# Gates taken from their PSUM banks, and a new order of work, in the seven-product ReGLU tiles of an attention and FFN kernel

## The chip, the core and the metric

One Trainium2 chip; the kernel runs on one of its cores. The metric is the time of one execution on the device in microseconds. The engines are TensorE (PE; PEld are its weight loads), VectorE (DVE), ScalarE (ACT), GpSimd (POOL) and SyncE (SP, which here issues transfers only). Each engine works through its own queue in the order written, and waits on semaphores of others. A transfer is issued from an engine's queue and lands later.

## The reference

Eight batches of eight heads, 576 positions of 64 numbers, attention that is causal by blocks of 64, and then a ReGLU feed-forward layer on all 4608 rows of 512 numbers, with 1536 hidden units:

```python
pos = np.arange(S)
mask = (pos[:, None] // 64) >= (pos[None, :] // 64)
scores = np.where(mask, q @ k.T * D ** -0.5, -1e9)
attn = softmax(scores)                       # per batch and head
x = (attn @ v).transpose(0, 2, 1, 3).reshape(B * S, H * D)
gate = np.maximum(x @ w_gate, 0.0)
val = x @ w_val
return (gate * val) @ w_out
```

## The kernel before, in words

**Tiles.** The 4608 rows go through the feed-forward layer as nine tiles of 512 columns: tiles 0 to 7 are the first 512 positions of the eight batches, tile 8 holds the 64 last positions of each. While tile j is in the feed-forward layer, the attention of the next batch runs between its matmuls. Tiles 0 to 2 have an order of their own that the change leaves alone. Tiles 3 to 6 share one text, `ORDER_3_6`; tiles 7 and 8, which have no attention beside them, have `ORDER_7` and `ORDER_8`. `program(j)` (L1324) turns each token of such a text into instructions; the order of tokens is the order on every engine's queue. No planner runs: order, banks and the sharing between engines are tables written out in the file.

**Seven products.** From tile 3 on a pair of hidden quarters (128 units each, two per pair) is computed with Winograd's form of Strassen's method: seven products of half size instead of eight. Token `pNw` is product w of pair N (L1363, four matmuls of 256 columns in two tokens). Products 1, 6, 5, 3 go to one PSUM bank (`w_`), 7 and 4 to another (`v_`), 2 to a third (`x_`). Between products the running sums are taken out: `pNa`, `pNu`, `pNw` are ScalarE copies of a bank to SBUF (L1385), `pNd`, `pNe`, `pNc` are VectorE additions of a bank to such a copy (L1389). At the end the bank `w_` holds the gate of the upper half of the columns, the copy `a` that of the lower half, `u` and `w` the values. The two hidden products are

```python
elif what == "r":
    relu((n, "high"), st[n, "w_"])        # ScalarE, L1334: gate_sb <- bank
...
if gate is not None:                      # L1401, VectorE or GpSimd
    on(name).tensor_tensor(out=h[:, :, at], in0=split(gate), in1=val, op=AX.mult)
else:                                     # L1405, VectorE: max(gate, 0) * value
    nc.vector.scalar_tensor_tensor(out=h[:, :, at], in0=split(...), scalar=0.0, in1=val, ...)
```

`pNL` is the lower half (always L1405, both inputs in SBUF). `pNH` is the upper half: with a token `pNr` before it, the ReLU copies the gate to SBUF and L1401 multiplies; without it, L1405 reads the PSUM bank itself. GpSimd can only do the form of L1401.

**Other tokens.** `g`, `v`, `r`, `h` are hidden quarters without the seven products (512-column matmuls L1339, ReLU L1334, VectorE product L1435). `X`, `Y` are sums of the input halves that pairs need (L1171), `sQPKK` sums of hidden quarters (L1020), `U` sums of weights (L979, in tile 6 only). `M1` to `M7` are the seven output products of a tile (L1061, six tokens each) over all twelve quarters; `oa`, `ou`, `ow`, `oy` are their ScalarE copies (L1106), `od`, `oe`, `oc` VectorE additions (L1100), `S0` to `S3` and `P` the stores (L893), on ScalarE's queue. In tile 8 the last parts are halved (`oya`, `oyb`, `oca`, `ocb`, L1118; stores `Sa`, `Sb`, `Sya`, `Syb`, two 64-row blocks after another, on several queues, L906). For attention, `A` is a visit (scores of two heads, L631, in banks of all three pools), `E` its exponentials (t, u, f of 512 columns, L643, or s of 1024, L636), `C` zeroed corners (memset L1519 on GpSimd, L1516 on VectorE), `V` the products with v (L779, L793), `N` the normalisation (L716, L718, L725), `T` the transposing transfer of the result to `xT` (L862, SyncE's queue; `T3` also issues that of the last positions, L765), `K` and `k` the last keys, `l` and `w` loads of a later batch (GpSimd's queue, L509), `d0` to `d3` the transposing transfers of its q and k (SyncE's queue, L519, L524, L526). `l`, `w` and `d` are left out in tile 6.

**Banks and queues.** PSUM has eight banks: two tiles `sc` of two banks, of which a pair uses the first, one bank `one`, three banks `ffnp`. `PAIR_BANK`, `OUT_BANK` and `AV_BANK` say which pool each accumulation uses, `SLOTS` which buffer of the pool, one after the other. A bank's next user on TensorE waits until ScalarE and VectorE have read it. `ON_POOL` lists the operations that GpSimd does; the rest of their kinds fall to VectorE (`on`, L946).

Of the kernel before, what the change touches and what calls it, by code (L numbers as in the profile page):

```python
# [17 lines left out]
def kernel(  # L18
# [91 lines left out]
    ORDER_8 = """  # L110
        p01 p31 p01 p0a p17 p11*2 p1a X4 p07 p17 p07 p0w p06 p12 p06 p0u p12 p1c p16*2
        p04 p05*2 p0d p21 p1u p15*2 p31 p1w p1d p14*2 p1e p3a p04 p1L p0e p21 p2a p03*2
        p0r p0H p13 p02 p13 p1r p02 p0c P p1H p36 p26*2 p2u p27*2 p2w p41 p32 p25 p32
        p41 p4a p25 s0002 p0L s0102 p2d p3c p37*2 p3w p36 p3u p24*2 p2e p23*2 p2r p2H
        p34*2 p3e p35 p47 p35 p3d p22*2 p47 p2c p4w p3L p2L p42 p51*2 p5a p42 p33*2 p3r
        p3H p4c p46*2 p56 p44*2 p4u p4e p4L p56 p5u p57*2 p5w p45*2 p4d p55*2 p5d p54*2
        p5e M2 p52 p43 p52 p5c p5L p53 p43 p4r p4H p53 p5r p5H M1*2 M2 M1*4 M2*4 s0202
        s1002 s1202 oa s2002 s2202 M6*2 M7 s2102 M6*4 s1102 M7 s0302 s2302 M7*4 ou oca
        Sa M5*5 ocb s1302 Sb ow M5 od M4 S2 M4*3 M3*3 oya Sya M4*2 oe S1 M3*3 oyb Syb
# [25 lines left out]
        (4, 2): ('one', 'sc', 'ffn'),  # L145
        (4, 3): ('ffn', 'sc', 'ffn'),
# [2 lines left out]
        (5, 2): ('one', 'sc', 'ffn'),
        (5, 3): ('ffn', 'sc', 'ffn'),  # L150
# [2 lines left out]
        (6, 2): ('one', 'sc', 'ffn'),
        (6, 3): ('ffn', 'sc', 'ffn'),
# [12 lines left out]
        (8, 5): ('ffn', 'ffn', 'sc'),  # L167
# [1649 lines left out]
```

## Time and profile before

| | |
|---|---|
| time, median of 3 runs | 345.14 us (344.94 to 345.31) |
| the profiled execution's own time | 344.71 us |
| its span | 342.8 us, granted TensorE clock 0.997 |
| TensorE busy | 332.7 us (97%) |
| VectorE, GpSimd, ScalarE busy | 233.1, 216.7, 210.8 us |

Read the busy shares with the stages in mind: tiles 3 to 6 take some 35.7 us each (tile 4 from about 174.5 to 210.2 us, tile 5 to 245.8), tile 7 runs from about 281.4 and tile 8 from about 309.3 us. Times in the views are from the start of the span; an operation's duration overlaps the next one's start on its engine, so the rate of a full queue is read from starts, not from durations. Idle time in square brackets is that of the engine before the row, with what released it.

### The profile page before, as it was taken

The numbers are of one execution on the slowest core, as the hardware profiler recorded it, in microseconds if no ns is written. First come the engines' busy times: TensorE is split into PE (matmuls) and PEld (weight loads), VectorE is DVE, ScalarE is ACT, GpSimd is POOL, SyncE is SP. The second block draws the span as 40 slices with busy tenths as digits, with TensorE's granted clock in tenths as the row PEclk, the third lists the DMA queues.
The fourth block names the chain that finished last, engine by engine and source line by source line (L and its number), as shares of the span: only waits on it lengthen the run. The fifth ranks groups of instructions, "written<-read, shape, count | busy, mean of one in ns | idle before, by whom it ended". The sixth has DMA issues, their size and how long they took to land.

```text
span 342.8 us, 8917 instructions
## 1 busy us (share of the span) xinstructions
PE 332.7 (97%) x3477; PEld 233.8 (68%) x3518; DVE 233.1 (68%) x540; ACT 210.8 (61%) x344; POOL 216.7 (63%) x272
## 2 busy tenths in 40 slices
...
GB/s 242 294 351 371 368 230 238 240 163 155 187 197 137 144 158 137 165 143 121 111 165 120 130 116 153 128 137 118 138 33 2 33 122 12 2 31 94 33 0 122
DMA packets 155337, 50.06 MB, mean 146 GB/s; under 512 B 134496, under 2 KB 151648, under 8 KB 155296
## 3 DMA queue, kind: packets, MB, share of 16 engines
...
## 4 chain that ended last, share of the span: by engine, by line
PE 88%; issue 4%; DVE 2%; ACT 2%; POOL 2%; POOLq 0%; DVEq 0%; ACTq 0%
PE ffnp L1179 16%; PE ffnp L1363 9%; PE ffnp L1339 8%; PE sc L1363 8%; PE sc L1061 6%; PE ffnp L1282 6%; PE ffnp L1061 6%; PE one L1363 5%; PE one L1061 4%; PE sc L631 3%; PE one L631 2%; PE one L779 2%; PE ffnp L779 2%; PE one L1179 2%; PE sc L779 1%
## 5 line engine op out<-in xcount | busy, mean ns | idle before, releaser
L636 ACT ACTIVATE attnT<-sc 128x1024 bf16<-128x1024 f32 x56 | 56.7, 1036 | 0.0
L1189 ACT ACTIVATE gate_sb<-ffnp 128x512 bf16<-128x512 f32 x35 | 20.6, 599 | 27.3 <-PE ffnp L1179 24.4
L1179 PE MATMUL ffnp<-xT,wg 128*128 128x512 bf16 x130 | 36.2, 379 | 0.6
L1061 PEld LDWEIGHTS <-stage 128*128 128x128 bf16 x336 | 32.0, 98 | 4.1 <-issue 0.2
L1363 PEld LDWEIGHTS <-stage 128*128 128x128 bf16 x288 | 27.3, 98 | 7.8
L779 PEld LDWEIGHTS <-attnT 128*128 128x128 bf16 x640 | 26.3, 98 | 7.7 <-DVE xnat L718 1.2
L1179 PE MATMUL ffnp<-xT,wv 128*128 128x512 bf16 x108 | 31.3, 380 | 0.2
L1199 DVE TENSOR_TENSOR hT<-gate_sb,ffnp 128x512 bf16<-128x512 bf16 x28 | 19.2, 684 | 14.9 <-PE ffnp L1179 12.0
L1389 DVE TENSOR_TENSOR ob<-ffnp,ob 128x512 f32<-128x512 f32 x29 | 19.8, 684 | 12.6 <-ACT ob L1385 12.6
L509 POOL DMA_DIRECT2D v_bf<-in_v_dram x30 | 24.3, 829 | 6.0 <-PE sc L793 3.1
L1061 PEld LDWEIGHTS <-hT 128*128 128x128 bf16 x252 | 24.2, 98 | 5.3 <-DVE hT L1405 1.1
L1363 PEld LDWEIGHTS <-wg 128*128 128x128 bf16 x224 | 21.9, 98 | 5.1
L1363 PEld LDWEIGHTS <-wv 128*128 128x128 bf16 x224 | 21.5, 98 | 5.3 <-ACT attnT L636 1.1
L1106 ACT COPY ob<-sc 128x512 f32<-128x512 f32 x13 | 7.6, 586 | 28.4 <-PE sc L1061 27.0
L1519 POOL MEMSET attnT<- 64x256 bf16 x34 | 10.2, 314 | 23.4 <-ACT attnT L636 16.0
L1282 PE MATMUL ffnp<-wo,hT 128*128 128x512 bf16 x91 | 23.1, 379 | 0.2
L1179 PEld LDWEIGHTS <-wg 128*128 128x128 bf16 x144 | 13.3, 98 | 13.8 <-issue 0.5
L1179 PEld LDWEIGHTS <-wv 128*128 128x128 bf16 x144 | 13.0, 98 | 14.3 <-issue 1.5
L1334 ACT ACTIVATE gate_sb<-ffnp 128x512 bf16<-128x512 f32 x30 | 17.6, 603 | 8.1 <-PE ffnp L1363 4.6
L509 POOL DMA_DIRECT2D q_bf<-in_q_dram x20 | 18.0, 908 | 5.0 <-DVE recip L752 4.0
L643 ACT ACTIVATE attnT<-one 128x512 bf16<-128x512 f32 (+1 forms) x28 | 15.0, 537 | 9.8 <-PE ffnp L631 8.4
L1020 POOL TENSOR_TENSOR stage<-hT,stage 128x512 bf16<-128x512 bf16 x15 | 17.4, 1167 | 4.2 <-DVE stage L1020 3.6
...
## 6 DMA issues: line engine op xcount, KB each, us to landing
...
stage<-in_moe_w_out_dram SPq DMA_DIRECT2D x6, 512.0 KB, 10.5
...
```

The source lines that it names most:

```text
L509: ins = nc.gpsimd.dma_start(dst, part_of)
L636: return lambda: nc.scalar.activation(at[:, :, lo : lo + 512], sc, AF.Exp, scale=scale)
L779: nc.tensor.matmul(av[:, p, :], at[:, col : col + 128], v_bf[b % 2][:, c, h, :], start=(p == 0), stop=(c == p), skip_group_check=True,)
L1061: nc.tensor.matmul(to, sums.of(c)[which][:, 128 * p : 128 * p + 128], right, start=first, stop=(c == 5), skip_group_check=True,)
L1179: nc.tensor.matmul(to, (wg, wv)[t][f // 4][:, c, 128 * (f % 4) : 128 * (f % 4) + 128], x[:, c], start=(c == 0), stop=(c == 3),)
L1189: nc.scalar.activation(gate_sb, gate, AF.Relu)
L1199: nc.vector.tensor_tensor(out=h, in0=gate_sb, in1=val, op=AX.mult)
L1282: nc.tensor.matmul(op, hT[f][:, 128 * s : 128 * (s + 1)], wo[f // 4][:, f % 4, n0:n1], start=(f == 0), stop=(f == 11),)
L1334: nc.scalar.activation(st[key], of, AF.Relu)
L1339: nc.tensor.matmul(to, (wg, wv)[t][f // 4][:, c, 128 * (f % 4) : 128 * (f % 4) + 128], x[:, c], start=(c == 0), stop=(c == 3),)
L1363: nc.tensor.matmul(st[key][:, 256 * k : 256 * k + 256], left[:, c, 128 * k : 128 * k + 128], right[:, c], start=new and (k, c) == (0, 0), ...
L1389: nc.vector.tensor_tensor(out=t, in0=st[n, of], in1=t, op=AX.add)
```

## The change

No function changes, only the tables.

1. The tokens `p1r` in tiles 3 to 6, `p1r`, `p3r`, `p4r`, `p5r` in tile 7 and `p1r`, `p4r`, `p5r` in tile 8 are gone. The upper halves of these pairs are now L1405 on VectorE with the gate's PSUM bank as an input; ReLUs that stay are `p3r` and `p5r` in tiles 3 to 6 (pair 2 had none before), `p0r` and `p2r` in tile 7, `p0r`, `p2r`, `p3r` in tile 8.
2. `ON_POOL` is shared out otherwise: in tiles 3 to 6 one upper half, two corners and two input sums leave GpSimd, and the hidden sums it takes are others; the weight sums, tile 7 and tile 8 change likewise.
3. Seven accumulations move from the `sc` banks to the `ffnp` banks, and many others change place. `SLOTS` is written anew from tile 3 on: `sc` has 126 places instead of 133, `ffnp` 233 instead of 226, `ob` 96 as before, `gate_sb` 65 instead of 76.
4. The three orders are written anew. In tiles 3 to 6 the second visit (`A1`) comes later, behind `p35`; the transposing transfers go out as T0 T1 d0 d1 d2 d3 T2 T3 instead of d0 d1 T1 T0 d2 d3 T2 T3; the loads `w4` and `w5` come earlier. In tile 7 `M7` comes ahead of most of `M1`. In tile 8 `M7` and `M1` come ahead of `M2`, and the store `Sb` moves behind `oya`.

The diff shows tile 3 for tiles 3 to 6 in the tables, grouped by tile:

```diff
--- before
+++ after
@@ -43,40 +43,39 @@
     SLOTS = {
...
     ORDER_3_6 = """
-        l0 A0 E0t E0u g0*2 p12 w0 p12 X5 X7 E0s E0f X6 X4 K g0*2 g1*2 p11*2 p1a g1*2
-        p17*2 p16*2 C00 C01 p1c k V00 N00 P v1*2 p1u p15*2 p1w p1d p14 V01 N01 p14 p1e
-        p1L v1*2 r0 r1 p13*2 p1r v0*2 h1 A1 E1t v0*2 h0 p21*2 E1s p22*2 w1 p27*2 p2a
-        p26*2 E1u l1 w2 p31 p1H l2 l3 p2c p31 g8 U05 l4 p2w p24*2 w3 s0002 p2u p2e p2L
-        l5 l6 p25 g8 p25 p2d C11 p3a p36*2 p32 p37*2 E1f C10 V11 l7 N11 U06 l8 p3u p35
-        p3w p35 p3d g8*2 r8 p23*2 p2H l9 p34*2 p3e p33*2 p3r p32 A2 E2t E2u p3c p3L v8*4
-        h8 p57 p51*2 p57 p52 E2s V10 N10 p5a p56*2 p5w d0 d1 T1 p5u s0202 p3H p52 p5c g9
-        p54*2 p5e l10 s1102 g9*3 p55*2 p5d C21 p5L s1002 E2f r9 s0302 s1202 A3 E3t v9
-        E3f U45 s0102 p53*2 p5r C20 v9 V21 v9 N21 v9 M1 h9 V20 M1*2 p5H s2102 s2002 E3s
-        C30 N20 U47 M1*3 M7*2 T0 d2 d3 E3u C31 V30 M7 V31 N30 T2 oa N31 s2202 s2302 M6*6
-        ou M7*3 ow M2 M5*5 M4 M5 M4*3 od S2 M4*2 oe S1 M2 U46 U43 M3 U07 w4 s1302 M3*5
-        M2*4 oc oy S0 w5 T3 U03
+        A0 E0t l0 X5 E0s E0u C01 X7 X6 g1*4 g0 E0f C00 K g0 p11*2 p1a g0 w0 w1 X4 p12*2
+        p1c g0 l1 w2 l2 p17*2 p16*2 k V00 N00 v1*4 P r1 p1u p1w h1 r0 p15*2 p1d V01 N01
+        p21 p14 p21 p2a p14 p1e v0 p27 v0*3 U05 h0 p1L p13 p26*2 p13 p1H p27 p22*2 p2c
+        p31 g8 p2w p24 p2u p24 p2e p31 p3a p25*2 p2d g8 p37*2 p3w p2L p36*2 p23*2 p2H
+        p34*2 g8 p3u p3e g8 r8 l3 l4 p35 w3 l5 l6 l7 A1 E1t l8 E1s U45 s0002 E1u C11 p35
+        p3d v8 E1f p32*2 p3c v8*3 h8 U06 s0202 p33*2 p3r p51*2 A2 E2u C10 V11 E2t p3L
+        p52*2 N11 p57*2 p5a p56 p5c V10 w4 p3H s1002 E2s s1102 p5w p56 p5u T0 N10 T1 d0
+        g9*2 C21 p54*2 p5e g9 E2f p55*2 p5d g9 U03 d1 d2 l9 l10 d3 r9 A3 E3u E3s p53*2
+        v9 p5L v9 s0102 s1202 v9*2 M1*2 p5r M1*2 E3f M1 M7 M1 h9 p5H s2002 C20 w5 E3t
+        C31 V21 C30 M7 V20 V30 N21 oa M6 s2202 M6*4 s2102 N30 N20 T2 M6 ou V31 N31 T3
+        M7*2 M2 M7*2 ow M5 M2 M5*5 od S2 M4*3 s0302 U46 M4*3 oe s1302 S1 U47 U07 M3
+        s2302 M3*5 M2 U43 oy M2*3 oc S0
     """
     ORDER_7 = """
-        p11 X5 X7 X6 X4 p01*2 p0a p02*2 p11 p1a p0c p12*2 p1c p06*2 p16*2 p07*2 p17*2
-        p0u p05*2 p21 p0w p1u p21 p04*2 p0d p0e p2a p15*2 p1w p1d p22 p03 p22 p03 p0r
-        p31 p14*2 p13*2 p1r p26 p31 p0L p27 p26 p27 p2c p1e p1H Y5 p1L p37*2 p0H s0002
-        s0202 s0102 p32*2 p2u p25 p3a p3c p36 p25 p36 p2w p24*2 p2d p2e p51*2 p3w p3u
-        p35*2 p3d p23*2 p2L p34*2 p5a p56 p33*2 p2r p2H p3e p3L p52 p57 p56 p41 p57 p41
-        p47 p3r p3H p52 p5c p42*2 p5u p55 p4a p4c p46*2 p47 p55 p5w p54 p5d p54 p5e M1
-        s1002 s1202 s1102 p4w p4u p44*2 p4e p45 p53 p45 p4d p53 M1 p5r P p4L p5L p5H
-        M2*2 M7 p43 M7 p43 p4r p4H s2002 s2202 s2302 M1*4 oa M2*4 M6*6 s2102 M7*4 ou
-        M5*3 ow M5*3 od S2 oc M4*6 s1302 s0302 oe M3*4 S1 Y7 Y6 M3*2 oy S0
+        p11 X5 X7 p01*2 p0a p21 p12 p11 X6 X4 p12 p1a p1c p07 p06*2 p0u p07 p02*2 p0c
+        p16 p05*2 p0w p0d p16 p1u p04*2 p0e Y5 p0L p17 p21 p2a p03 p17 p1w p15 p03 p15
+        p26 p14*2 p1d p31*2 p1e p1L p13 p0r p0H p3a p27 p22 p27 p2w p22 p2c p26 p13 p37
+        p1H s0002 s0202 p24*2 p36 p2u p2e p25 p37 p25 p51 p32 p36 p32 s0102 p51 p2d p23
+        p52 p2L p3c p3u p35*2 p23 p52 p3w p3d p34*2 p5a p5c p2r p56 p57 p56 p33*2 p5u
+        p3e p57 p41*2 p42*2 p4a p3H p2H s1002 p5w p3L p4c p47*2 p55 p46 p55 p5d p46
+        p54*2 p5e p4w p44 p4u p44 p4e p45*2 p4d p4L M1 s1102 p53 M7*2 p53 p43 M2 p43 M2
+        M1 p5L M1*4 M2*4 oa s1202 M6 p5H p4H s2002 s2202 s2302 M6*5 ou P s2102 M7*4 ow
+        oc s0302 M5*5 s1302 M5 od Y7 S2 M4*6 oe S1 M3*6 oy S0 Y6
     """
     ORDER_8 = """
-        p01 p31 p01 p0a p17 p11*2 p1a X4 p07 p17 p07 p0w p06 p12 p06 p0u p12 p1c p16*2
-        p04 p05*2 p0d p21 p1u p15*2 p31 p1w p1d p14*2 p1e p3a p04 p1L p0e p21 p2a p03*2
-        p0r p0H p13 p02 p13 p1r p02 p0c P p1H p36 p26*2 p2u p27*2 p2w p41 p32 p25 p32
-        p41 p4a p25 s0002 p0L s0102 p2d p3c p37*2 p3w p36 p3u p24*2 p2e p23*2 p2r p2H
-        p34*2 p3e p35 p47 p35 p3d p22*2 p47 p2c p4w p3L p2L p42 p51*2 p5a p42 p33*2 p3r
-        p3H p4c p46*2 p56 p44*2 p4u p4e p4L p56 p5u p57*2 p5w p45*2 p4d p55*2 p5d p54*2
-        p5e M2 p52 p43 p52 p5c p5L p53 p43 p4r p4H p53 p5r p5H M1*2 M2 M1*4 M2*4 s0202
-        s1002 s1202 oa s2002 s2202 M6*2 M7 s2102 M6*4 s1102 M7 s0302 s2302 M7*4 ou oca
-        Sa M5*5 ocb s1302 Sb ow M5 od M4 S2 M4*3 M3*3 oya Sya M4*2 oe S1 M3*3 oyb Syb
+        X4 p11 p07 p01 p12 p11 p01 p07 p12 p17*2 p1a p1c p16 p31 p0a p06*2 p21 p0w p04*2
+        p16 p0u p0e p05*2 p0d p1w p14*2 p21 p31 p1u p15 p1e p15 p1d p2a p3a p03*2 p0r
+        p1L p02*2 p0c p26*2 p2u P p13*2 p36 p1H p27*2 p2w p32*2 p36 p0L p0H s0002 s0202
+        p25*2 p2d p3u p37 p3c s0102 p24*2 p2e p37 p35*2 p3w p3d p23*2 p2r p22 p34*2 p41
+        p22 p3e p47 p2c p41 p4a p47 p4w p33 p42 p33 p51 p46 p42 p3L p2L p3r p3H p2H
+        s1002 s1102 p46 p51 p44 p4c p52 p57 p44 p4u p45 p4e p57 p45 p4d p5a p56*2 p52
+        p5c p5w p54 p5u p54 p5e p55*2 p5d p4L p5L p43*2 p4H M7 M1 M2*2 M1 p53 M7 p53 p5H
+        s2002 M1*4 oa M2*4 s1202 M6*2 s2202 M6*4 ou s2102 M7*4 oca s1302 ocb s2302 s0302
+        M5*4 Sa ow M5*2 od M4*2 S2 M4*2 M3*3 oya Sb Sya M4*2 oe S1 M3*3 oyb Syb
     """
...
     PAIR_BANK = {
         (3, 1): ('sc', 'sc', 'ffn'),
-        (3, 2): ('one', 'sc', 'ffn'),
-        (3, 3): ('ffn', 'sc', 'ffn'),
+        (3, 2): ('one', 'ffn', 'sc'),
+        (3, 3): ('ffn', 'sc', 'one'),
         (3, 5): ('ffn', 'one', 'ffn'),
-        (7, 0): ('ffn', 'one', 'one'),
+        (7, 0): ('ffn', 'ffn', 'one'),
         (7, 1): ('sc', 'sc', 'sc'),
         (7, 2): ('ffn', 'ffn', 'ffn'),
-        (7, 3): ('one', 'ffn', 'sc'),
-        (7, 4): ('ffn', 'one', 'ffn'),
-        (7, 5): ('sc', 'sc', 'ffn'),
+        (7, 3): ('one', 'sc', 'ffn'),
+        (7, 4): ('ffn', 'one', 'sc'),
+        (7, 5): ('sc', 'ffn', 'ffn'),
         (8, 0): ('one', 'sc', 'ffn'),
         (8, 1): ('ffn', 'ffn', 'sc'),
-        (8, 2): ('sc', 'one', 'sc'),
+        (8, 2): ('sc', 'sc', 'one'),
         (8, 3): ('ffn', 'ffn', 'ffn'),
-        (8, 4): ('sc', 'ffn', 'one'),
-        (8, 5): ('ffn', 'ffn', 'sc'),
+        (8, 4): ('sc', 'ffn', 'sc'),
+        (8, 5): ('ffn', 'ffn', 'one'),
     }
...
     ON_POOL = set(
-        33H 35H 3C00 3C01 3C10 3C11 3C20 3C21 3C30 3C31 3X4 3X6 3X7
-        3s0102 3s0202 3s0302 3s1302 3s2202 3s2302
-        70H 72H 7X4 7X5 7X6 7Y5 7Y7 7s0102 7s0202 7s0302 7s1002 7s1102 7s1202 7s1302 7s2302
-        80H 82H 83H 8s0002 8s0102 8s1002 8s1202 U03 U06 U07 U46
+        33H 3C01 3C10 3C11 3C20 3C21 3C30 3X4
+        3s0302 3s1002 3s1102 3s1302 3s2102 3s2202 3s2302
+        70H 72H 7X4 7X5 7Y7 7s0002 7s0102 7s0202 7s1002 7s1102 7s1202 7s2302
+        80H 82H 8X4 8s0102 8s0202 8s1002 8s1102 8s1202 8s2302 U05
...
-    OUT_BANK = {(3, 'v'): 'one', (3, 'w'): 'sc', (3, 'x'): 'ffn',
-        (7, 'v'): 'one', (7, 'w'): 'ffn', (7, 'x'): 'ffn',
-        (8, 'v'): 'sc', (8, 'w'): 'ffn', (8, 'x'): 'one'}
+    OUT_BANK = {(3, 'v'): 'ffn', (3, 'w'): 'ffn', (3, 'x'): 'ffn',
+        (7, 'v'): 'one', (7, 'w'): 'ffn', (7, 'x'): 'sc',
+        (8, 'v'): 'one', (8, 'w'): 'sc', (8, 'x'): 'one'}
...
-    AV_BANK = {0: ('one', 'one'), 1: ('sc', 'sc'), 2: ('ffn', 'one'), 3: ('ffn', 'sc')}
+    AV_BANK = {0: ('one', 'ffn'), 1: ('ffn', 'ffn'), 2: ('sc', 'sc'), 3: ('one', 'one')}
```

More of the change, by code (lines that the diff above doesn't have):

```diff
@@ L140 @@
         (3, 1): ('sc', 'sc', 'ffn'),
[L141 to L142 removed]
+        (3, 2): ('one', 'ffn', 'sc'),
+        (3, 3): ('ffn', 'sc', 'one'),
         (3, 5): ('ffn', 'one', 'ffn'),
         (4, 1): ('sc', 'sc', 'ffn'),
[L145 to L146 removed]
+        (4, 2): ('one', 'ffn', 'sc'),
+        (4, 3): ('ffn', 'sc', 'one'),
         (4, 5): ('ffn', 'one', 'ffn'),
         (5, 1): ('sc', 'sc', 'ffn'),
[L149 to L150 removed]
+        (5, 2): ('one', 'ffn', 'sc'),
+        (5, 3): ('ffn', 'sc', 'one'),
         (5, 5): ('ffn', 'one', 'ffn'),
         (6, 1): ('sc', 'sc', 'ffn'),
[L153 to L154 removed]
+        (6, 2): ('one', 'ffn', 'sc'),
+        (6, 3): ('ffn', 'sc', 'one'),
         (6, 5): ('ffn', 'one', 'ffn'),
[L156 removed]
+        (7, 0): ('ffn', 'ffn', 'one'),
         (7, 1): ('sc', 'sc', 'sc'),
         (7, 2): ('ffn', 'ffn', 'ffn'),
[L159 to L161 removed]
+        (7, 3): ('one', 'sc', 'ffn'),
+        (7, 4): ('ffn', 'one', 'sc'),
+        (7, 5): ('sc', 'ffn', 'ffn'),
         (8, 0): ('one', 'sc', 'ffn'),
         (8, 1): ('ffn', 'ffn', 'sc'),
[L164 removed]
+        (8, 2): ('sc', 'sc', 'one'),
         (8, 3): ('ffn', 'ffn', 'ffn'),
[L166 to L167 removed]
+        (8, 4): ('sc', 'ffn', 'sc'),
+        (8, 5): ('ffn', 'ffn', 'one'),
     }
```

34 lines of the change are left out of this document (16 added, 18 removed).

## The prediction

> **What bounds the kernel now.** I read the page's busy table first, then a table of windows by tile, then TensorE's own list in the last tiles, because only there does it stop. The page:
>
> ```profile
> span 342.8 us, 8917 instructions
> PE 332.7 (97%) x3477; PEld 233.8 (68%) x3518; DVE 233.1 (68%) x540; ACT 210.8 (61%) x344; POOL 216.7 (63%) x272
> ```
>
> and the windows, which fall on tiles 4, 5, 7 and 8 (columns: window, length, then busy us and instruction counts of PE, PEld, DVE, ACT, POOL, then the clock):
>
> ```profile
> 175.00:211.00 36.00, 35.74 (x425) 27.58 (x422) 25.34 (x57) 24.80 (x41) 28.59 (x36) 1.00 1.30 132
> 211.00:247.00 36.00, 35.74 (x417) 27.61 (x419) 25.33 (x58) 24.94 (x42) 26.83 (x34) 1.00 1.16 137
> 282.00:308.00 26.00, 25.77 (x236) 22.71 (x234) 20.92 (x36) 15.13 (x27) 15.24 (x14) 1.00 0.06 21
> 308.00:343.00 35.00, 29.80 (x267) 25.67 (x265) 24.09 (x44) 15.99 (x29) 10.52 (x10) 0.97 0.21 61
> ```
>
> TensorE is busy 35.74 of 36 us in tiles 4 and 5; the other engines have 7 us and more to spare in each. Nothing can be gained in tiles 3 to 6, whose matmuls the change keeps. The time TensorE does lose is in the last two tiles (its list in order of time there; matmuls of 256 columns that follow each other start 0.109 apart, so a row of x7 hands over after 0.76):
>
> ```profile
> 301.13 0.27 PE L1061 MATMUL ffnp<-wo,hT 128*128 128x256 bf16 x1
> ...
> 301.64 1.81 PE L1061 MATMUL ffnp<-wo,hT 128*128 128x256 bf16 x15 [0.23 <-DVE hT L1405]
> ...
> 325.61 0.60 PE L1363 MATMUL ffnp<-perm,stage 128*128 128x256 bf16 x4
> 326.18 0.60 PE L1363 MATMUL ffnp<-perm,wv 128*128 128x256 bf16 x4
> ...
> 328.14 0.93 PE L1061 MATMUL ffnp<-wo,hT 128*128 128x256 bf16 x7
> 329.38 1.81 PE L1061 MATMUL ffnp<-wo,hT 128*128 128x256 bf16 x15 [0.31 <-DVE hT L1405]
> ...
> 333.69 1.47 PE L1061 MATMUL ffnp<-stage 128*128 128x256 bf16 x12
> 335.51 1.03 PE L1061 MATMUL sc<-stage,hT 128*128 128x256 bf16 x8 [0.35 <-ACT ob L1106]
> ...
> 337.03 0.60 PE L1061 MATMUL sc<-stage,hT 128*128 128x256 bf16 x4
> 337.66 0.82 PE L1061 MATMUL ffnp<-wo,stage 128*128 128x256 bf16 x6
> ```
>
> The gaps beyond 0.109 are 0.40 in tile 7 (M1, waiting for VectorE's p5L), and in tile 8 0.14, 0.48 (M1 again), 0.51 (M4) and 0.19: with one of 0.03 some 1.35. The two tiles together lose 1.8 us: the most that this change can win there, since the matmuls stay. The clock gives nothing either: it stands at 1.00.
>
> **Prices.** From the groups of the trace from tile 3 on:
>
> ```profile
> L1334 ACT ACTIVATE gate_sb<-ffnp 128x512 bf16<-128x512 f32 x30 | 17.6, 603 | 8.1 <-PE ffnp L1363 4.6 <-PE ffnp L1339 3.2
> L1401 POOL TENSOR_TENSOR hT<-gate_sb,ob 128x512 bf16<-128x512 bf16 x8 | 9.3, 1163 | 11.7 <-ACT gate_sb L1334 11.5
> L1405 DVE SCALAR_TENSOR_TENSOR hT<-one,ob 128x512 bf16<-128x512 f32 x4 | 2.8, 691 | 0.0
> L1020 POOL TENSOR_TENSOR stage<-hT,stage 128x512 bf16<-128x512 bf16 x15 | 17.4, 1167 | 4.2 <-DVE stage L1020 3.6
> L1020 DVE TENSOR_TENSOR stage<-hT 128x512 bf16<-128x512 bf16 x26 | 10.5, 419 | 0.6 <-POOL hT L1401 0.5
> L1171 POOL TENSOR_TENSOR perm<-xT,perm 128x512 bf16<-128x512 bf16 x10 | 11.6, 1158 | 5.3 <-DVE perm L1171 4.8
> L1171 DVE TENSOR_TENSOR perm<-xT 128x512 bf16<-128x512 bf16 x4 | 1.8, 450 | 0.0
> L1519 POOL MEMSET attnT<- 64x256 bf16 x32 | 9.6, 315 | 15.6 <-ACT attnT L636 8.2 <-ACT attnT L643 6.8
> ```
>
> Rates and hand-offs, from ScalarE's queue in tile 5 and from the last output of tile 8:
>
> ```profile
> 233.25 0.60 ACT L643 ACTIVATE attnT<-one 128x512 bf16<-128x512 f32 x1 [0.17 <-PE one L631]
> 233.75 1.02 ACT L636 ACTIVATE attnT<-sc 128x1024 bf16<-128x1024 f32 x1
> 234.65 0.60 ACT L1334 ACTIVATE gate_sb<-ffnp 128x512 bf16<-128x512 f32 x1
> ...
> 329.24 1.29 DVE L1401 TENSOR_TENSOR hT<-gate_sb,q_bf 128x512 bf16<-128x512 bf16 x2
> ...
> 338.58 0.42 DVE L1118 COPY ob<-ffnp 128x256 f32<-128x256 f32 x1 [0.21 <-PE ffnp L1061]
> ```
>
> In a full queue ScalarE spends 0.50 per 512 columns and 0.90 per 1024 (starts 233.25, 233.75, 234.65), VectorE about 0.60 (two in 1.29). The last six matmuls, from 337.66, are through at 338.31; VectorE starts 0.27 later. In the other direction the matmul at 329.38 follows p5L, which ended at 329.32 (behind it 329.24 starts in the same queue), by 0.06.
>
> **The change, part by part.**
> 1. Eleven ReLUs go: one in each of tiles 3 to 6, four in tile 7, three in tile 8. The upper half then reads the gate's bank (L1405 with a PSUM operand, 0.69 as in `hT<-one,ob`) instead of the copy (L1401). ScalarE saves 0.60 each; VectorE pays the same where it made the product before. 35H in tiles 3 to 6 (and its like) and 83H leave GpSimd: 1.16 there becomes 0.69 on VectorE. The bank is held until VectorE, not ScalarE, has read it, which is why seven banks move from the two-bank pool to the three-bank pool.
> 2. GpSimd per tile 3 to 6: minus one upper half, two corners, X6, X7, plus one sum net: 19 operations (15.3 us) become 15 (12.4). VectorE gains 0.69 + 2 × 0.45, two corners of at most 0.31 each, less 0.42: up to 1.8 us. Its 25.3 busy us in 36 become about 27: no bound, its idle time (in the M stage) covers it. In tile 6 three more weight sums go over to VectorE (its idle time is 9 us there), tile 7 loses three GpSimd operations, tile 8 gets two more: GpSimd's busy time falls by 11.6 + 3.5 + 3.5 − 2.3, some 16 us.
> 3. The order is new, and every cost lies here. I lined up each tile by hand: tokens at 0.218 us of TensorE (four 256-column matmuls of a token pair, or two plus two), each engine's queue in written order at the rates above. Tiles 3 to 6: visit A1 moves from 8.05 to 14.36 us after A0, so five exponentials and the first copies of pair 5 meet. ScalarE begins A1's exponentials at 15.42 and is then full: E1s, E1u, E1f, p3r, E2u, E2t, p5a, E2s, p5w are .91 + .48 + .91 + .50 + .49 + .48 + .48 + .91 + .59 = 5.75, done at 21.17, handed on at 21.22; the product that overwrites this bank (second p56) is due at 21.12. That is 0.10. A2 waits for the hidden product h8 (0.27 + 0.69 + 0.06 = 1.02 against 0.97 of work between): 0.05. A3 behind p5e meets 0.05, though part of it lies behind the first. I take 0.15 per tile, 0.6 in four. Bounds: 0, as in tiles 4 and 5 now, and 0.9. Everything else there came out with slack, six places with under 0.1.
> 4. Tile 7: the first M7 waits for p4e in the bank it takes: p5e starts at 16.84, p4e at 17.44, ends 18.13, handed on at 18.19 against 17.88: 0.31. M1's second column waits 0.06 for p5L. 0.37 against 0.40 to 0.46 now: −0.09.
> 5. Tile 8: p55 waits 0.19 for copy p5u; M1 waits 0.18 for p5L (p5c at 16.84, then p5e, p5d, p4L, and p5L ends at 16.84 + 4 × 0.60 + 0.69 = 19.93) instead of 0.47. M4's wait for copy `ow` goes, because of these rows (ScalarE's queue, tile 8):
>
> ```profile
> 333.36 1.47 ACTq L906 DMA_DIRECT2D out_dram<-ob  x2
> 334.87 0.59 ACT L1106 COPY ob<-sc 128x512 f32<-128x512 f32 x1 [1.49 <-DVE stage L1020]
> ```
>
> `ow` stood behind two store issues of 1.47 together; now only Sa is ahead of it and Sb comes behind `oya`. M3 then waits 0.15 for `od` (1.02 against four tokens, 0.87) and 0.19 for `oya`. Together 0.71 against 1.35: −0.64. What is late next is the tail: Sb's issue now lies among the last ones, +0.05 (0 to 0.3).
> 6. SyncE's queue, tiles 3 to 6: d0 d1 T1 T0 d2 d3 T2 T3 becomes T0 T1 d0 d1 d2 d3 T2 T3. Tile 5 shows the prices:
>
> ```profile
> 223.68 3.11 SPq L519 DMA_TRANSPOSE qTm<-q_bf  x1
> 231.13 2.29 SPq L519 DMA_TRANSPOSE kTm<-k_bf  x1
> 233.88 2.50 SPq L862 DMA_TRANSPOSE xT<-xnat  x2
> 236.48 1.19 SPq L524 DMA_TRANSPOSE qTt<-q_bt  x1
> 237.78 1.77 SPq L526 DMA_TRANSPOSE kTt<-k_bt  x1
> 239.65 2.52 SPq L862 DMA_TRANSPOSE xT<-xnat  x2
> ...
> DMA to landing us min/median/max: 2.4/3.0/4.3
> ```
>
> (the last line belongs to the view of tile xT.) T1 is ready at about 21.6 after A0; then d0 and d1 at 1.9 to 3.1 each, d2 1.2, d3 1.2 to 1.8, T2 1.2, and T3 lands 2.4 to 4.3 after its start: between 33.8 and 38.3, centrally 35.5 to 36. The next tile's matmuls first need it 1.5 us into that tile, at about 37.0. I book nothing, with the high end, 1.3 us a tile, kept for the range. The earlier weight and V loads run on GpSimd's queue, which has 2.9 us more room.
>
> Sum: +0.6 − 0.09 − 0.64 + 0.05 = −0.1 us on the profiled execution's 344.71 (span 342.8 and 1.9 around it): 344.6. The median of the runs shown is 345.14, 0.43 above, so 345.0. Two runs of this kernel can be told apart at about 0.2%, 0.7 us; this is no change.
>
> **One rule beside the rows.** VectorE and GpSimd block each other:
>
> ```profile
> 228.02 1.34 DVE L1405 SCALAR_TENSOR_TENSOR hT<-ob,ob 128x512 bf16<-128x512 f32 x1
> ...
> 227.65 1.17 POOL L1401 TENSOR_TENSOR hT<-gate_sb,ob 128x512 bf16<-128x512 bf16 x1
> ```
>
> The VectorE operation that reads two SBUF tiles takes 1.34, not 0.69, and gets going when GpSimd's ends at 228.82. The Trainium skill, "SBUF — State Buffer", section "Who interferes with whom", says that such an operation needs GpSimd's port, that whoever issues first holds it for the whole instruction, and that one SBUF input makes no conflict. The rows here agree (851 ns mean for `ob,ob`); by it the new upper halves, with a PSUM input, are free of it and the two-input lower halves are not.
>
> **Rivals.**
> - *No stall in tiles 3 to 6.* Tiles 4 and 5 lose nothing now, with a ScalarE queue that also runs without a gap from 233.25 on. Then −0.64 − 0.09 + 0.05 = −0.7: 344.4. Against it: the run that p56 waits for is 5.75 us long. Chance 0.2, half of it beyond −0.2%.
> - *Tiles 4 to 6 start late: slower.* SyncE issues in order; if d0 and d1 both take 3 us, T3 lands past 37.0 and TensorE's gate product waits for xT. At 0.7 us mean over three tile starts this is +2.1 on 345.0: 347.1. It decides once T1 is handed out after about 23 us, or d0 and d1 exceed 5 us together. For it: 3.11 and 2.29 above. Against it: in tile 5 the last two xT transposes were issued at 239.65, 28 us into its window, and did no harm. Chance 0.17.
> - *Port conflict in tile 7, or pinches that add up: slower.* VectorE's p2L (two SBUF inputs) is due at 10.68, GpSimd's second sum at 10.72, 1.16 long. If GpSimd starts first, p2L ends a microsecond late in a queue that is full, p3d and p4e move, and tile 7 loses some 0.6; six places of under 0.1 slack in tiles 3 to 6 may cost as much again: +0.6 to +1.2, 345.6 to 346.2. By the skill's rule above this is what would happen whenever GpSimd is first. Chance 0.23.
>
> **Numbers.** Forecast 0.4 (344.7 to 345.6), rivals 0.2, 0.17, 0.23. Beyond −0.7 us: half the first rival and some of the forecast's lower edge with a shorter tail, 0.18. Beyond +0.7: the second rival and most of the third, 0.35. The rest 0.47. The range from 344.0 (no stall, and tile 7's gone too) to 347.1 (late tile starts) leaves out some 2 in 10.
>
> **What would show it.** Right: no gap of TensorE over 0.15 us in tiles 3 to 6; `ow` starts 0.2 after its product; M1's wait in tile 8 about 0.2; ScalarE about 6.6 us less busy, GpSimd some 16 less. Wrong: L1339 or L1363 waiting for xT at a tile's start, kTm issued past 30 us after A0, an L1405 of over 1.2 us in tile 7, or TensorE short of 35.6 us in 36 in tile 4.

## The result, and the profile after

| | before | after |
|---|---|---|
| median | 345.04 us (344.63 to 345.31) | 348.36 us (347.89 to 348.67) |
| ratio | | 1.0096, 95% interval 1.0078 to 1.0113 |
| profiled execution, its span | 344.71, 342.8 us | 348.48, 346.7 us |
| TensorE busy | 332.7 us | 333.3 us |

The change made the kernel slower by 3.3 us, 1%, outside the range and on the side of the second rival. (Lines of the file lie two further up after the change: L1363 is L1361 and so on.) The windows of the kernel after, tiles 4 and 5 and the two last stretches:

```profile
175.00:211.00 36.00, 34.02 (x400) 26.43 (x404) 25.36 (x60) 23.14 (x38) 25.59 (x32) 1.00 1.17 123
211.00:247.00 36.00, 34.02 (x400) 26.25 (x402) 24.54 (x60) 23.73 (x39) 24.82 (x31) 1.00 1.31 126
...
282.00:308.00 26.00, 25.92 (x238) 22.86 (x237) 23.55 (x41) 12.10 (x22) 12.83 (x12) 1.00 0.13 39
308.00:346.00 38.00, 34.00 (x306) 29.40 (x304) 27.17 (x46) 15.45 (x28) 14.20 (x13) 1.00 0.21 63
```

Tiles 4 and 5, which lost nothing before, have 1.7 us less of TensorE each. Where it stands still is one line of its table of waits (what it waited for, us in total, times, longest) and one place in its list, at the start of tile 5:

```profile
PE ffnp L1337 <- DMA xT<-xnat: 3.4, 2, 1.7
```

```profile
213.37 0.82 PE L1337 MATMUL ffnp<-xT,wg 128*128 128x512 bf16 x3
215.87 0.59 PE L1337 MATMUL ffnp<-xT,wg 128*128 128x512 bf16 x2 [1.68 <-DMA xT<-xnat]
```

Three of the four matmuls of the first `g1` run, the fourth needs the last quarter of `xT` and starts 1.84 us late; tile 4 loses 1.85 us in the same way. That quarter is brought by `T3`, which leaves late: SyncE's queue during tile 4 (each row is the issue; A0 of this tile starts at 175.0):

```profile
198.13 1.51 SPq L860 DMA_TRANSPOSE xT<-xnat  x1
199.85 1.79 SPq L517 DMA_TRANSPOSE qTm<-q_bf  x1
201.82 3.57 SPq L517 DMA_TRANSPOSE kTm<-k_bf  x1
205.49 1.20 SPq L522 DMA_TRANSPOSE qTt<-q_bt  x1
206.79 2.21 SPq L524 DMA_TRANSPOSE kTt<-k_bt  x1
209.09 2.59 SPq L860 DMA_TRANSPOSE xT<-xnat  x2
211.77 1.78 SPq L763 DMA_TRANSPOSE xTt<-xtail  x1
```

`T1` goes out at 198.13, 23.1 us after A0, and the four transposes of the next batch stand behind it. The normalised results for `T2` and `T3` were there at 206.2 and 207.3, but the queue reaches `T3` at 210.41. It lands at 215.82: the view of `xT` there gives 3.7, 4.6 and 5.4 us from issue to landing for `T2` and `T3` (least, median, most), and 6.3 for `T3` of tile 3:

```profile
DMA to landing us min/median/max: 3.7/4.6/5.4
```

In tile 3, whose late `T3` makes the first of the two stalls, the queue itself ran as forecast:

```profile
160.59 1.19 SPq L860 DMA_TRANSPOSE xT<-xnat  x1
162.00 1.71 SPq L517 DMA_TRANSPOSE qTm<-q_bf  x1
163.88 4.01 SPq L517 DMA_TRANSPOSE kTm<-k_bf  x1
...
170.59 2.53 SPq L860 DMA_TRANSPOSE xT<-xnat  x2
```

```profile
DMA to landing us min/median/max: 6.3/6.3/6.3
```

The last line is the landing of `T3` alone. A0 of tile 3 starts at 139.04, so `T1` went out 21.6 us after it, and `T3`, at 171.90, left 3.1 us ahead of the next A0. TensorE asks for its data at 176.4; with 4.3 us to landing, the longest that the prediction allowed, it would have been there at 176.2. It landed at 178.2.

At the start of tile 6 `T3` is no earlier than in tile 4 (247.97, the next A0 at 250.2), but there no load of q runs beside it (`l0` is left out in tile 6; the expectation of e3 below calls this the start of tile 7), it lands in 3.1 us and TensorE loses nothing. Two stalls of 1.85 us are 3.69 of the 3.8 us by which the span grew. The rest: tiles 3 to 6 lose 0.66 us more together (tile 7 starts at 285.85 instead of 281.46: 4.39 − 3.69 and 0.04 of an earlier difference), tiles 7 and 8 take 0.62 less up to the last row of matmuls (285.85 to 341.43 against 281.46 to 337.66), and from there to the landing of the last store it takes 0.07 more (345.59 − 341.43 against 341.75 − 337.66).

Runs more than 1.5% above the fastest of their kernel, at a lower mean clock, are left out of the ratios below: three of ten in e1 (351.23, 352.25 and 356.80 us), one each in e2, e3, e4 and e8, and two of the kernel before.

### The profile page after: what moved, and what is told of

The parts are those of the page before. It is cut to its first block, busy times and chain, and to the rows that moved or that the text cites. A ratio compares the mean times of both kernels' runs of the same rounds, so it can differ in the third digit from the quotient of the medians.

```text
span 346.7 us, 8899 instructions
## 1 busy us (share of the span) xinstructions
PE 333.3 (96%) x3481; PEld 234.1 (68%) x3518; DVE 238.8 (69%) x560; ACT 203.5 (59%) x333; POOL 200.9 (58%) x252
## 4 chain that ended last, share of the span: by engine, by line
PE 83%; DVE 5%; DMA 4%; ACT 3%; issue 3%; POOL 1%; POOLq 0%; DVEq 0%; ACTq 0%
PE ffnp L1177 16%; PE ffnp L1059 13%; PE ffnp L1361 10%; PE sc L1361 8%; PE ffnp L1337 7%; PE ffnp L1280 6%; PE one L1361 5%; DMA xT<-xnat 3%; PE sc L629 3%; PE one L777 2%; PE one L629 2%; PE ffnp L777 2%; PE one L1177 1%; PE one L1059 1%; PE sc L777 1%
## 5 line engine op out<-in xcount | busy, mean ns | idle before, releaser
L634 ACT ACTIVATE attnT<-sc 128x1024 bf16<-128x1024 f32 x56 | 57.5, 1040 | 0.0
L1517 POOL MEMSET attnT<- 64x256 bf16 x26 | 8.0, 310 | 64.4 <-ACT attnT L641 31.3
L1104 ACT COPY ob<-ffnp 128x512 f32<-128x512 f32 x23 | 13.7, 596 | 44.5 <-PE ffnp L1059 44.5
L1177 PE MATMUL ffnp<-xT,wg 128*128 128x512 bf16 x130 | 36.2, 379 | 0.6
L1187 ACT ACTIVATE gate_sb<-ffnp 128x512 bf16<-128x512 f32 x35 | 20.5, 599 | 26.9 <-PE ffnp L1177 21.2
L1361 PEld LDWEIGHTS <-stage 128*128 128x128 bf16 x288 | 27.2, 98 | 8.8 <-issue 1.9
L1361 PEld LDWEIGHTS <-wv 128*128 128x128 bf16 x224 | 21.9, 98 | 5.5 <-issue 0.8
L1018 POOL TENSOR_TENSOR stage<-hT 128x512 bf16<-128x512 bf16 x19 | 22.0, 1172 | 4.5 <-DVE hT L1399 2.2
L1361 PEld LDWEIGHTS <-wg 128*128 128x128 bf16 x224 | 21.4, 98 | 3.6
L1383 ACT COPY ob<-ffnp 128x512 f32<-128x512 f32 x26 | 15.5, 596 | 11.9 <-PE ffnp L1361 11.3
L1098 DVE TENSOR_TENSOR ob<-ffnp,ob 128x512 f32<-128x512 f32 (+1 forms) x17 | 11.2, 659 | 16.3 <-PE ffnp L1059 15.2
L1337 PE MATMUL ffnp<-xT,wg 128*128 128x512 bf16 x56 | 18.3, 380 | 3.4 <-DMA xT<-xnat 3.4
```

The source lines that it names most:

```text
L634: return lambda: nc.scalar.activation(at[:, :, lo : lo + 512], sc, AF.Exp, scale=scale)
L1018: (eng or nc.vector).tensor_tensor(out=of(part), in0=a, in1=b, op=op)
L1177: nc.tensor.matmul(to, (wg, wv)[t][f // 4][:, c, 128 * (f % 4) : 128 * (f % 4) + 128], x[:, c], start=(c == 0), stop=(c == 3),)
L1187: nc.scalar.activation(gate_sb, gate, AF.Relu)
L1337: nc.tensor.matmul(to, (wg, wv)[t][f // 4][:, c, 128 * (f % 4) : 128 * (f % 4) + 128], x[:, c], start=(c == 0), stop=(c == 3),)
L1361: nc.tensor.matmul(st[key][:, 256 * k : 256 * k + 256], left[:, c, 128 * k : 128 * k + 128], right[:, c], start=new and (k, c) == (0, 0), ...
```

## The experiments

Two theories of the stall: "queue", the new order of SyncE's queue sends `T3` out too late; "landing", `T3` lands late because it shares the DMA engines with the first load of q (`l0`) and the stores. A third, "rest", puts the cost on the gates, the banks and the sharing. The kernel before ran beside each of them; its median was 344.67 to 344.98.

| run | median, us | ratio to before, 95% |
|---|---|---|
| e1 change, d0 d1 first | 344.98 of seven, 347.77 of all ten | 1.0038 (0.9999 to 1.0077) |
| e2 before, T0 T1 first | 347.06 | 1.0057 (1.0039 to 1.0075) |
| e3 change, l0 later | 345.94 | 1.0026 (1.0009 to 1.0044) |
| e10 change, fewer stores | 346.58 | 1.0053 (1.0035 to 1.0071) |
| e11 change again | 348.03 | 1.0107 (1.0089 to 1.0125) |
| e7 change, three tokens moved | 345.78 | 1.0030 (1.0013 to 1.0048) |
| e4 before, gates only | 350.36 | 1.0152 (1.0130 to 1.0175) |
| e5 before, sharing only | 354.17 | 1.0293 (1.0238 to 1.0349) |
| e6 before, new tiles 7 and 8 | 344.59 | 0.9986 (0.9977 to 0.9996) |
| e8 e6, Sb early | 344.77 | 0.9998 (0.9988 to 1.0008) |
| e9 e8, six operations to GpSimd | 348.54 | 1.0115 (1.0100 to 1.0131) |
| e12 e8, sixteen small writes | 343.63 | 0.9964 (0.9951 to 0.9976) |

### e1: only the order of SyncE's queue put back

```diff
-  ... p5w p56 p5u T0 N10 T1 d0 g9*2 ... p5d g9 U03 d1 d2 l9 l10 d3 r9
+  ... p5w p56 p5u d0 d1 T0 N10 T1 g9*2 ... p5d g9 U03 d2 l9 l10 d3 r9
```

> The changed kernel, with d0 and d1 put ahead of T0 and T1 again in tiles 3 to 6; nothing else differs. Theory 'queue': in the changed kernel T1 goes out 23.3 us after A0 of tile 4 (198.13), d0 and d1 stand behind it and take 5.5 us, so T3 leaves at 210.41, 2.0 us before the next A0, and its landing at 215.82 holds TensorE for 1.85 us, twice. Then this kernel has T3 out by 34 us after A0, no wait for xT at a tile start, and 344.3 to 345.1 us. Theory 'landing': not the queue but the load of q beside it (l0, issued 209.22, landed 214.34) makes T3 take 5.4 us to land; T3 still runs beside it, and half of the loss or more stays: 346.2 to 348.4. Theory 'rest' (gates, banks, sharing cost the time): 348.4, unchanged.

```profile
189.55 3.73 SPq L517 DMA_TRANSPOSE qTm<-q_bf  x1
194.24 2.25 SPq L517 DMA_TRANSPOSE kTm<-k_bf  x1
196.58 3.33 SPq L860 DMA_TRANSPOSE xT<-xnat  x2
200.00 1.20 SPq L522 DMA_TRANSPOSE qTt<-q_bt  x1
201.44 1.19 SPq L524 DMA_TRANSPOSE kTt<-k_bt  x1
204.14 2.91 SPq L860 DMA_TRANSPOSE xT<-xnat  x2
```

SyncE works off `d0` and `d1` while it would otherwise wait for `T1`, and in tile 4 `T3` leaves at 205.43, five us sooner (1.85 of them the stall that is gone). In tile 3 it leaves at 171.24, only 0.7 us sooner than in the change, but lands in 4.6 us instead of 6.3, 0.5 us ahead of its use. The profiled execution (344.63) has no wait for `xT`. But of the ten runs only four lie between 344.63 and 344.98, three at 346.70 to 349.01 and three above 351. With the old order of this queue the loss can vanish, as "queue" said; it does not do so in every run, and the start of tile 4 has no reserve. None of the six longer runs was traced.

### e2: the new order alone, in the kernel before

```diff
-  ... p5a p56*2 p5w d0 d1 T1 p5u ... M1*3 M7*2 T0 d2 d3 E3u
+  ... p5a p56*2 p5w T0 T1 d0 d1 p5u ... M1*3 M7*2 d2 d3 E3u
```

> The kernel before, with T0 and T1 ahead of d0 and d1 in tiles 3 to 6; nothing else differs. 'Queue': it gets the loss that the changed kernel has, T3 out some 2 us before the next A0 and 1 to 2 us of waiting for xT at two or three tile starts: 347 to 349. 'Landing': here the load of q goes out at 206.6 and has landed at 211.6, so T3, however late it leaves, lands in about 3 us; 345.0 to 345.8. 'Rest': 345.0.

347.06 us, all but one run from 345.35 to 348.66: the four moved tokens cost the old kernel 2 us with nothing else changed. Gates, banks and sharing are not needed for it. It does not decide between the two theories. "Landing" counted on a load of q that is through at 211.6; in the traced run it went out at 208.40 and landed at 212.94, so `T3`, issued at 209.96, had it and the stores beside it and took 6.3 us to land (5.6 in tile 3). The two are links of one chain: the order sends `T3` out later, among transfers beside which it lands late. The profiled execution was the longest (351.05) and shows more than the stall. TensorE's list and two windows behind it (the number ahead of the last two is the granted clock):

```profile
213.34 0.27 PE L1363 MATMUL ffnp<-xT,wg 128*128 128x256 bf16 x1
216.32 0.80 PE L1363 MATMUL ffnp<-xT,wg 128*128 128x256 bf16 x3 [2.71 <-DMA xT<-xnat]
```

```profile
216.40:219.40 3.00, 2.78 (x13) 1.59 (x14) 0.00 (x0) 0.00 (x0) 2.91 (x3) 0.50 0.03 7
219.60:222.60 3.00, 3.00 (x36) 2.15 (x35) 1.43 (x4) 2.22 (x5) 2.94 (x6) 0.98 0.28 91
```

After 2.87 us of standing still the clock is 0.50 for 3 us, 13 matmuls where 36 follow in the next 3 us. After the 1.84 us of the changed kernel it stayed at 1.00.

### e3 and e10: what makes T3 land late

```diff
-  A0 E0t l0 X5 E0s ... p1c g0 l1 w2 l2
+  A0 E0t X5 E0s ... p1c g0 l0 l1 w2 l2
```

> The changed kernel, with the first load of q (l0) moved from the start of the tile to just ahead of l1; SyncE's order stays that of the change. 'Queue': T3 still leaves 2.0 us before A0, the stalls of 1.85 us stay to more than half: 347.2 to 348.4. 'Landing': T3 lands in about 3.1 us, as at the start of tile 7 in the changed kernel (247.97 to 251.04, where no load of q runs), TensorE has its data when it asks, and the kernel takes 344.5 to 345.2. 'Rest': 348.4.

```profile
PE ffnp L1337 <- DMA xT<-xnat: 0.4, 1, 0.4
```

345.94 us, between the two expectations. In tile 4 `T3` leaves at 208.51 and lands in 3.3 us instead of 5.4; there the stall is gone with SyncE's order unchanged. In tile 3 it still takes 5.1 and 0.55 us are lost. So the load of q beside it is a part of the cause, as "landing" said, but not all of it.

In e10 the tokens `S0`, `S1`, `S2` are left out of tiles 3, 4 and 5:

```diff
     ONLY = {
+        'S0': (6, 7, 8), 'S1': (6, 7, 8), 'S2': (6, 7, 8),
```

> The changed kernel without the stores S0, S1 and S2 of tiles 3, 4 and 5, so three quarters of the output of these tiles are not written; SyncE's order and l0 are those of the change. It asks what else besides l0 makes T3 land late. If the stores do (in tile 3 T3 still took 5.1 us with l0 moved away): T3 lands 3 to 4 us after its issue, the stalls at the starts of tiles 4 and 5 shrink to under 0.6 each, 344.4 to 345.8. If l0 does alone: landing stays at 5 us and more, both stalls at 1.3 to 1.9, 347 to 348.4.

```profile
PE ffnp L1340 <- DMA xT<-xnat: 1.1, 1, 1.1
```

346.58 us, again between the two. Without these stores `T3` of tile 4 lands in 3.5 us and tile 5 starts without a wait; in tile 3 it takes 5.4 us with no store beside it, and tile 4 loses 1.24. Either neighbour taken away clears the start of tile 5; at the start of tile 4 the stall of 1.85 us only shrinks, to 0.55 and 1.24. What sets the landing of `T3` in tile 3 stays open.

The change itself once more, beside e9 and e10:

> The changed kernel itself once more, beside the other two on their chip: 347.9 to 348.7 as before, with two stalls of some 1.85 us for xT; a spread over more than 1 us would say that the landing of T3 differs from run to run.

346.68 to 348.90, with stalls of 1.00 and 0.67 in the profiled run of 346.68. The landing differs from run to run, and the loss with it.

### e4 and e5: the gates alone, the sharing alone

```diff
-  ... p13*2 p1r v0*2 ...  E1u l1 w2 p31 p1H l2
+  ... p13*2 p1H v0*2 ...  E1u l1 w2 p31 l2
   (tile 7: p1r, p3r, p4r, p5r and tile 8: p1r, p4r, p5r removed)
```

> The kernel before with only the gates changed: the eleven ReLU tokens that the change drops are dropped, their upper halves read the PSUM bank; in tiles 3 to 6 the upper half of pair 1 stands where its ReLU stood. My sum booked this part at nothing: 344.6 to 345.2, no new gap of TensorE over 0.2 us, ScalarE 6.6 us less busy. Rival: a bank is held until the busier VectorE has read it, TensorE waits for banks in tiles 7 and 8: 345.4 to 346.5.

```profile
PE sc L630 <- DVE hT L1404: 2.9, 4, 0.7
```

350.36 us. The scores of `A1` take the bank in which pair 1 keeps its gate. ScalarE's ReLU used to free it; now it is free when VectorE has come to the product, and the scores wait 0.89 us longer than their switch in each of four tiles. Tile 7 loses 0.95 at a bank in the same way, tile 8 0.50 and 0.20: 5.2 us together. (This profiled execution has besides a wait of 2.8 us ahead of tile 3 for which the runs of 349.75 to 350.88 leave no room.) The second expectation was right in kind and too low.

```diff
-  ON_POOL = the list of before
+  ON_POOL = the list of the change
```

> The kernel before with only the list of GpSimd's operations taken from the change. My sum: no engine becomes a bound, 344.6 to 345.4, GpSimd some 16 us less busy, VectorE some 8 more. Rival: the order of before was fitted to the old sharing, and X6, X7, the corners and the second upper half on VectorE delay its copies at places with under 0.1 us of slack: 0.2 to 0.5 us a tile, 345.8 to 347.

```profile
PE ffnp L778 <- POOL attnT L1518: 5.1, 4, 1.3
```

354.17 us: the products with v wait 1.44 us in each of tiles 3 to 6 for a zeroed corner that stands on GpSimd's queue behind the sums given to it there, one of which itself waits 3.20 us for a product of VectorE. That makes 5.8 of the 9.4 us; tiles 7 and 8 lose some 3.0 us more than in the kernel before, and the rest stays open. The rival was right that the old order does not fit the new sharing, but put it at 0.2 to 0.5 us a tile. GpSimd is 14 us less busy over the kernel, and TensorE waits for it all the same.

### e6, e8, e9, e12: the last tiles, and what the tail did with them

e6 has tiles 0 to 6 as before and 7 and 8 as changed (orders, banks, sharing, with the buffers renamed at the seam).

> Tiles 0 to 6 as before, tiles 7 and 8 (orders, banks, sharing, their seven missing ReLUs) as in the change. My sum gives these two tiles -0.64 - 0.09 + 0.05 = -0.7; in the changed kernel's trace their gaps add up to 1.1 us against 1.8: 344.3 to 344.6. If the gates taken from the banks cost something of themselves, or the tail eats the gain, 344.9 to 345.6.

344.59 us, a gain of 0.3. TensorE's last matmul came 0.94 us sooner (337.26 against 338.20), but the span stayed at 342.8. Sb was suspected, and moved:

```diff
-  M5*4 Sa ow M5*2 od M4*2 S2 M4*2 M3*3 oya Sb Sya M4*2 oe
+  M5*4 Sa ow Sb M5*2 od M4*2 S2 M4*2 M3*3 oya Sya M4*2 oe
```

> Tiles 0 to 6 as before, 7 and 8 as in the change, but Sb right behind ow instead of behind oya. In the run with Sb late the last matmul began at 337.26, 0.94 earlier than before (338.20), but the last store landed at 341.67 against 341.75: its issue at 338.17 was followed by 3.5 us to landing, against 2.65. Theory 'Sb in the tail ate it': with Sb's blocks out 2 us earlier the last store lands 2.7 to 2.9 us after its issue, the span is 342.0 to 342.3 and the time 343.8 to 344.1. If the long landing has another cause, 344.4 to 344.7 as with Sb late.

That fell: 344.77, the span again 342.9. The DMA view of its end (from 337.5 us on: the queues, then the last four issues with the time to landing) shows the difference from the kernel before, whose last four took 2.6, 2.7, 2.5 and 2.6:

```profile
q14 instruction: 1, 0.01, 0.4%
issues: line engine op xcount, KB each, median us to landing
out_dram<-ob SPq DMA_DIRECT2D x1, 128.0 KB, 2.7
out_dram<-ob POOLq DMA_DIRECT2D x1, 128.0 KB, 3.1
out_dram<-ob ACTq DMA_DIRECT2D x1, 64.0 KB, 3.4
out_dram<-ob SPq DMA_DIRECT2D x1, 64.0 KB, 3.5
```

One 8 KB load of instructions lies among the last stores, and the last ones land 0.9 us later. Such loads came, among others, when VectorE had reached its 448th, 574th and 703rd row; before ends at 698, e6 and e8 at 706. Two ways to have it elsewhere. e9 takes six operations from VectorE:

```diff
   ON_POOL = set("""
+    U43 U45 U47 6s1102 6s1002 6s1202
```

> The run with Sb early (tiles 0 to 6 as before, 7 and 8 as in the change, Sb right behind ow) with six VectorE operations of tile 6 handed to GpSimd: the weight sums U43, U45, U47 and the hidden sums s1002, s1102, s1202. Why: in the two runs with the new last tiles the last store landed 3.5 us after its issue instead of 2.6, and among its packets lies one of 8 KB of the queue that loads instructions, at 340.1 and 340.3, when VectorE had come to its 703rd row of the trace, 128 behind the load before; the kernel before ends at 698 rows and has no such load. Theory 'code load in the tail': with VectorE below 703 rows the load is gone, the last store lands 2.6 us after its issue, the span is 342.0 to 342.2 and the time 343.7 to 344.1. Rival, the tail has another cause: the span stays at 342.8, 344.4 to 344.8. GpSimd has room in tile 6 (20 of 35 us busy); if the sums come late there, a gap of TensorE in the output products shows it.

The last stores did land 2.5 and 2.7 us after their issue, but the sums blocked GpSimd's queue ahead of a corner in tile 6, as in e5:

```profile
273.92 0.73 PE L767 MATMUL one<-v_bf,attnT 128*128 128x65 bf16 x10 [3.21 <-POOL attnT L1507]
```

```profile
274.00:276.00 2.00, 2.00 (x20) 1.33 (x20) 0.85 (x4) 0.00 (x0) 1.86 (x3) 0.50 0.03 8
```

3.4 us lost, again with the clock at 0.50 behind it: 348.54, so the time itself decides nothing about the tail. e12 makes VectorE's program longer instead:

```diff
+    if j == 6 and t == "N31":
+        for _ in range(16):
+            nc.vector.memset(spare, 0.0)      # 128 x 2, read by nobody
```

> The run with Sb early and nothing handed to GpSimd, plus sixteen writes of two numbers to a tile that nobody reads, on VectorE where it stands idle in the output stage of tile 6 (276.1 to 278.4). They bring VectorE to its 703rd row some 16 rows sooner, at about 329 instead of 340. Theory 'code load in the tail': the 8 KB load moves from 340.3 to 327 to 331, the last store lands 2.5 to 2.7 us after its issue at about 338.3, the span is 341.9 to 342.1 and the time 343.7 to 344.0, faster than both kernels. If the load sits where it did, or the landing stays at 3.5 us without it, 344.5 to 344.8. If the sixteen writes take more than the 2.3 us of idle time, 0.1 to 0.5 more, with a gap of TensorE at the start of tile 7.

```profile
275.69 1.96 DVE L1778 MEMSET spare<- 128x1 uint32 x16
```

```profile
out_dram<-ob ACTq DMA_DIRECT2D x2, 64.0 KB, 2.4
out_dram<-ob SPq DMA_DIRECT2D x1, 128.0 KB, 2.6
out_dram<-ob POOLq DMA_DIRECT2D x1, 128.0 KB, 2.7
out_dram<-ob SPq DMA_DIRECT2D x1, 64.0 KB, 2.6
```

The load now comes at 327.6, the last store lands in 2.6 us, the span is 341.7 and the time 343.63 us, 0.36% (0.24 to 0.49) less than the kernel before: faster than both. From the start of tile 7 to TensorE's last matmul the new tiles save 0.6 us in the change and 0.9 in e6, e8 and e12, and the tail no longer gives it back; 0.2 us more of e12's traced run lies ahead of tile 7.

### e7: the change with three tokens moved

The edits of e1, e3 and e8 in the changed kernel.

> The changed kernel with three tokens moved: d0 d1 ahead of T0 T1 and l0 ahead of l1 in tiles 3 to 6, Sb right behind ow in tile 8. Theory 'queue and landing together': T3 lands 3 us or more before TensorE asks, no wait for xT in any run, so the spread of the run with d0 d1 alone (344.6 to 349.0) closes; tiles 3 to 6 keep some 0.14 us each, the last tiles and the earlier Sb give back 0.7 to 0.9 and more of the tail: 344.2 to 344.8. If the order of SyncE's queue and l0 are not the whole cause, some runs stay above 346.

345.78 us, with nine of ten runs within 345.38 to 346.67 and one at 348.15: steadier than e1, but above the 344.2 to 344.8 expected and not below before. The profiled execution still loses 0.80 to `xT` at the start of tile 4, and in tile 7 the third rival came up. VectorE's p2L and GpSimd's second sum in the order of time (start, duration), first in the changed kernel, then in e7:

```profile
296.58 0.68 DVE L1403 SCALAR_TENSOR_TENSOR hT<-ob,k_bf 128x512 bf16<-128x512 f32 x1
296.64 1.64 POOL L1018 TENSOR_TENSOR stage<-stage,hT 128x512 bf16<-128x512 bf16 x1
```

```profile
293.48 1.16 POOL L1018 TENSOR_TENSOR stage<-stage,hT 128x512 bf16<-128x512 bf16 x1
...
293.70 1.48 DVE L1403 SCALAR_TENSOR_TENSOR hT<-ob,k_bf 128x512 bf16<-128x512 f32 x1
```

In the first VectorE begins 0.06 us ahead and GpSimd takes 1.64 instead of 1.16; in the second a copy that ScalarE began 0.27 us late had shifted VectorE, GpSimd is first, and VectorE takes 1.48. Three gaps of 0.11 to 0.16 us follow on TensorE. The Trainium skill, "SBUF — State Buffer", section "Who interferes with whom", says that issue order decides who blocks; this pair of runs shows both outcomes of the same two instructions.

## Why the prediction was wrong, point by point

**What failed is step 6, SyncE's queue**, booked at nothing and worth 3.69 us, and in it the landing of `T3`. `T3` landed after 6.3 us (tile 3) and 5.4 (tile 4), where the bounds had 2.4 to 4.3, taken from a queue in which `T3` left ahead of the stores and of `l0`. The other links came as forecast. In tile 3 `T1` was out 21.6 us after A0, `d0` and `d1` took 5.7 us together, inside the bounds for the two, and `T3` left at 32.9. In tile 4 `T1` was out at 23.1, which holds the 1.85 us of the stall that the tile starts with, and `T3` left at 35.4. By these rows, with 4.3 us to landing, `T3` of tile 3 would have been 0.2 us early and that of tile 4 0.7 us late (an estimate). Beside `l0` or the stores it took longer; why it did so in tile 3 with either of them gone stays open.

The bounds of the time at which `T3` lands, 33.8 to 38.3 us after A0, do not follow from the terms listed for them, which with an issue of 1.2 us for `T1` give 32.6 to 37.5; the sum did not use them. It went by the middle of each span, though they are links of one chain with 1 us of reserve at its end. The second rival described the mechanism and its sign, and both of its conditions were met (`d0` and `d1` over 5 us together in both tiles; `T1` past 23 us only in the tile that the first stall had delayed). It looked for the cause in the issues and left out the neighbours of `T3`; its price of 0.7 us at three starts was 1.85 at two, and the top of the range, 347.1, took 2.1 us for it where its own high end, 1.3 us at three starts, gave 3.9.

**The other terms held.** Tiles 3 to 6: 0.6 forecast, 0.66 measured. In tiles 4 to 6 it is 0.09 behind copy p5w and 0.05 ahead of A3, as forecast; A2 lost nothing. (The product that takes the bank of p5w is p54; the prediction calls it the second p56.) Tiles 7 and 8: −0.73 forecast, −0.62 measured: M1 in tile 8 still lost 0.37 instead of 0.18, M7 in tile 7 0.25 instead of 0.31. The tail: +0.05 forecast, +0.07 measured; in the change the 8 KB load of instructions comes at 330.9, ahead of it.

**Steps 1 and 2 were right only within the new order.** In the change no gap of TensorE from tile 3 on ends with a product that reads a gate's bank, or with GpSimd. Alone, in the old order, they cost 5 and 9 us (e4, e5). "The bank is held until VectorE has read it" was written down without asking who takes that bank next, and "no engine a bound" looked at busy shares where a place in a queue decided.

**First rival** (no stall in tiles 3 to 6): refuted, 0.66 us stay in them, and 0.68 in e1. **Third rival**: its port conflict did not come in the profiled execution of the change, and did in that of e7.
